# First batch's x in seven pieces, tables and weights held behind it, and other transfer figures in the program that orders the instructions

## The chip, the cores and the metric

The kernel runs on one core of one Trainium2 chip. The core has a matrix engine (TensorE, PE in the profile, with its weight loads as PEld), a vector engine (VectorE, DVE), an activation engine (ScalarE, ACT), a general engine (GpSimd, POOL), and a sequencer (SyncE, SP) that issues every transfer of this kernel; sixteen DMA engines move the data. The metric is the time of one execution on the device in microseconds, as the median of the runs.

## The reference

The first half is a dynamic convolution: every position gets a softmax over 7 taps for each of 8 heads, and adds the 7 last rows of x with these weights. The second half is a Fourier mixing (real part of a two-dimensional transform over positions and channels), a normalization and an MLP of width 768.

```python
batch, seq, d_model = (8, 4224, 192)     # x is (8, 4224, 192), weight_gen (8, 4224, 8, 7)
w = softmax over the 7 taps of weight_gen
out = np.einsum('bshk,bskhg->bshg', w, x_unf)        # x_unf: the 7 rows up to s, 8 heads of 24
X = np.fft.fft(np.fft.fft(x, axis=1), axis=2)        # x is now out
u = x + np.real(X)
un = (u - mean) / np.sqrt(var + 1e-06)               # over the 192 channels
ch = np.maximum(un @ w_ch1, 0.0) @ w_ch2             # 192 -> 768 -> 192
return u + ch
```

## The kernel before, in words

A sequence of 4224 positions is laid out as 128 partitions of 33 rows, so that the transform over positions splits into one of 128 and one of 33 points. The tile x_sb holds 45 such rows of 192 channels for one batch: the 33 and, twice, 6 rows that the taps reach back to. All eight batches use the same x_sb, one after another.

For a batch b the work goes through these steps.

- **conv(b).** Softmax of the tap weights (tile w, maxima and sums in wm), then chunk by chunk: chunk 0 to 7 holds four rows (two from the low half of x_sb and two from the high half), chunk 8 one row. A chunk needs 7 products of x rows with weights wp (tiles pr_b_c_k for chunk c and tap k) and their sum u. Products are made by DVE, some by POOL (POOL_TAPS) and some by ACT (ACT_TAPS). In batch 0 the sums of chunks 0, 1, 3, 5 and 7 are made by PE, which multiplies each product with the identity into a PSUM tile pa; these products share three buffers (tag g2). The other chunks are added by POOL. POOL then folds u into sm, PE multiplies sm with the table f1 (pg), DVE makes gt of it, and gt is written to DRAM (g_d).
- **transform(b)** reads g_d back (g2, printed as g), multiplies it with the tables te and to (pp), and copies the result to pq. **mix(b, g)** multiplies pq with the table cs (eo) and adds it to u.
- **norm(b, g)** normalizes a group g of four rows (un), splits it into two halves of 16 bits (hl), and has it transposed by a DMA (ht<-hl, from group 3 of batch 0 on). From batch 1 on, a second DMA copies 64 partitions of it to the other half of the partitions (hd<-ht, 64 KB).
- **mlp(n)** with n = 9b + g: the first products ph = ht x w1, in 16-bit parts. In the middle of a group come products with only 64 rows of w1l, which use ht and hd side by side. Behind them relu (hh), the second products po = hh x w2, and the addition to u that is written out.

For batch 0, x comes in the pieces of X_PIECES (line 32): a row (a0, a1, b0, b1) stands for two transfers of rows a0 to a1 and b0 to b1, and need_x(c) issues the next rows of the list until chunk c has what it needs. In batch 0 the program asks for x of chunk 8 and 0 first, then for the rest of the weights w, then for chunks 1 and 3, and then load_consts issues the tables f1, te, to, cs and some zeros; load_weights, the MLP's weights, comes behind conv(0).

That order is not what the chip sees. The code records all instructions on a tape, and plan(tape) puts them in an order for each engine: it walks through all of them with a cost for each (cost), a wire that all transfers share, the tiles' buffers, and the places that the program gave them, several times forward and back, and keeps the best walk. In cost, a transfer (lane "sp") has three numbers: the time that SP is busy with it, the time until it is done, and the time that it takes on the wire; the walk adds up the last of them in `wire`. A hold (`held(op)`) tells the planner that what is recorded under it comes behind op on op's engine; it is no wait on the data. emit writes the instructions out in the order found; each engine works through its list in order, and waits where an operand or a buffer isn't ready. All instructions carry the line of emit, 408, so they are told apart by their tiles.

Of the kernel before, what the change touches and what calls it, by code (L numbers as in the profile page):

```python
# [28 lines left out]
NC = 8  # L29
KW = 144  # L30
XR = 45
X_PIECES = [(0, 7, 45, 45), (7, 9, 36, 45), (9, 13, 32, 36), (13, 17, 28, 32), (17, 21, 24, 28), (21, 24, 24, 24)]
TRI = 4
QUICK = 3
PAIRED = 9
# [13 lines left out]
POOL_TAPS = {(0, 0): (5, 6), (0, 1): (5, 6), (0, 3): (6,), (1, 0): range(7), (1, 1): range(7)}  # L49
DVE_ADDS = {(1, c): 1 for c in range(2, NC)}  # L50
HOLD3 = 3
WIRE = 0.7

F32_GROUPS = 7
ACT_ROWS = 4
# [136 lines left out]
def cost(op):  # L192

    lane, reads, writes = op.lane, op.reads, op.writes
    count = lambda ap: int(np.prod([n for _, n in ap.ap[1:]]))
    out = writes[0]
    n = max(map(count, reads + writes))
    if lane == "pe":
        n = count(out)
        t = 2 * max(112 if 64 < n <= DH else 56, 0.855 * n) if reads[0].dtype == F32 else max(55.8, 0.417 * n + 2.4)  # L200
        if op.visit:
            return t / 2, t + 178
        return t, t + 178
    if lane == "sp":
        if op.kw.get("transpose"):
            return 1450, 2000 + 1.2 * n, 1.09 * n
        size, run = BYTES[out.dtype], min(together(ap) for ap in reads + writes)
        return 400, 2000 + WIRE * count(out) * size, out.ap[0][1] * count(out) / run * (0.5 + 0.0023 * run * size)
    if lane == "dve":
        t = 150 + (6.27 if op.call == "reciprocal" else 1.042) * n + (60 if len(reads) == 3 and n < 512 else 0)  # L210
        return t - 83, t
    if lane == "pool":
        t = 183 + (1.92 if out.dtype == F16 else 2.13) * n
        return t - 45, t
    t = 190 + (0.833 if out.ap[-1][0] == 1 else 1.666) * n + 90 * (len(reads) - 1)
    return (t + 100, t + 90) if len(writes) > 1 else (t - 95, t)


def plan(tape):
# [51 lines left out]
    def walk(rank, rows, back=False):  # L271

        to, left = (before, after) if back else (after, before)
        left, ready, span = [len(n) for n in left], [0.0] * len(ops), [None] * len(ops)
        uses = {name: len(set(users[name])) for name in row_of}
        ends, placed, heads = defaultdict(float), {}, {row: 0 for row in rows}
        spare = {row: [(-1e3, i) for i in range(homes[names[0]].bufs)] for row, names in rows.items()}
        free, waiting = {lane: 0.0 for lane in HOP}, {lane: set() for lane in HOP}
        order, table, wire = [], None, 0.0
        half, stays = None, defaultdict(int)  # L280
        taken, wanted = defaultdict(int), {}
        for v in visits:
            stays[v] += 1
        door = set() if back else {span[0] for span in enters.values()}
        for k, n in enumerate(left):
            if n == 0:
                waiting[lanes[k]].add(k)

        def claim(name):

            kind = homes[name].use
            if kind == "fft" and taken["fft"] >= FFT:
                return BANKS
            group = family[name]
            return sum(n for g, n in wanted.items() if g != group)

        def opens(k):

            t = ready[k]
            for name in tiles[k]:  # L300
                if name not in placed:
                    row = row_of[name]
                    if back or row != SHARED:
                        while rows[row][heads[row]] in placed:
                            heads[row] += 1
                        if rows[row][heads[row]] != name:
                            return None
                    if not spare[row] or (row == SHARED and not back and len(spare[row]) <= claim(name)):
                        return None
                    t = max(t, min(spare[row])[0] + HOP[lanes[k]] + (ROOM if row == SHARED else 0))  # L310
            if k in door:
                if len(spare[SHARED]) < 3:
                    return None
                t = max(t, sorted(spare[SHARED])[2][0] + HOP["pe"] + ROOM)
            return t

        for _ in ops:
            at = [(max(free[lane], t), rank[k], k) for lane, ks in waiting.items()
                  for t, k in ((opens(k), k) for k in ks) if t is not None]
            if not at:  # L320
                return None
            if half and stays[half]:
                at = [a for a in at if lanes[a[2]] != "pe" or visits[a[2]] == half] or at
            now = min(at)[0]
            lane = next(lane for lane in HOP if any(t == now and lanes[k] == lane for t, _, k in at))
            k = min((r, k) for t, r, k in at if t == now and lanes[k] == lane)[1]
            if kinds[k] and kinds[k] != table:
                now, table = now + 1283, kinds[k]
            if lane == "pe":
                if visits[k] != half:  # L330
                    now, half = now + VISIT, visits[k]
                stays[half] -= 1
            waiting[lane].remove(k)
            order.append((now, k))
            busy, done, *load = costs[k]
            free[lane], end = now + busy, now + done
            if load and not back:
                wire = max(wire, now + 1000) + load[0]
                end = max(end, wire + 1000)
            span[k] = now, end  # L340
            for name in tiles[k]:
                row = row_of[name]
                if name not in placed:
                    spot = min(spare[row])
                    placed[name] = spot[1]
                    if row == SHARED:
                        taken[homes[name].use] += 1
                        group = family[name]
                        if group in groups:
                            if group not in wanted:  # L350
                                wanted[group] = 6
                            wanted[group] -= 1
                            if not wanted[group]:
                                del wanted[group]
                    spare[row].remove(spot)
                uses[name] -= 1
                ends[name] = max(ends[name], end)
                if not uses[name]:
                    spare[row].append((ends[name], placed[name]))
                    if row == SHARED:  # L360
                        taken[homes[name].use] -= 1
            for j, sync in to[k].items():
                loose = lanes[j] == lane and (lane == "pe" or not sync)
                ready[j] = max(ready[j], now if loose else end + HOP[lane if back else lanes[j]] + (SLACK if lanes[j] != lane else 0))
                left[j] -= 1
                if left[j] == 0:
                    waiting[lanes[j]].add(j)
        return max(end for _, end in span), span, order, placed
# [91 lines left out]
def tile_dynconv_fnet_mlp(  # L460
# [12 lines left out]
    real, nc = tc.nc, Tape()  # L473
# [236 lines left out]
    def conv(b):  # L710
# [13 lines left out]
        def need_x(c):  # L724
            need = {r + k + (0 if r < NT else K - 1) for r in rows_of(c) for k in range(K)}
            while not rows_x.issuperset(need):
                a0, a1, b0, b1 = next(pieces)
                for lo, hi in ((a0, a1), (b0, b1)):
                    if lo < hi:
                        nc.sync.dma_start(x_sb[:, lo:hi, :], x[b, :, lo:hi, :])  # L730
                        rows_x.update(range(lo, hi))

        def need_taps(c):
# [14 lines left out]
        if b == 0:  # L748
            with held(loads[0].ins):
                need_x(NC)  # L750
            with held(tops[0].ins):
                nc.vector.memset(x_sb[:, 7:37:29, 0:1], 0.0)
            first = len(nc.ops)
            need_x(0)
            holds.append((first + 1, 1e9, nc.ops[first]))
            tap_step(0, 4)
            need_x(1)
            need_x(3)
            load_consts()
            if -1 in WARM:  # L760
                keep_warm(pst("fft", [P, P], F32, "warm_x"), WARM[-1])
        groups = [(NC, 0), (1, 2), (3, 4), (5, 6), (7,)] if b == 0 else [(c,) for c in range(NC + 1)]
# [191 lines left out]

    state, us, products = {}, {}, []
    last_tile, last_pg, last_product, last_fold, last_gt, last_g2, last_pp = {}, {}, {}, {}, {}, {}, {}
    last_pq, last_mix, last_up, g2_load = {}, {}, {}, {}
    pending = {}
    total = B * NG

# [234 lines left out]
    last_word, last_split, last_lo, last_bn, last_ph, scales = [], [], {}, {}, {}, []  # L1195
    add(0.0, 1.0, conv(0))
    run(0.5)
    loaded = load_weights()
    run()
    def queue(ins, *calls):  # L1200
        with held(ins):
# [115 lines left out]
```

## Time and profile before

| | us |
|---|---|
| three runs | 1092.83, 1090.03, 1091.94 |
| median | 1091.94 |
| the profiled execution | 1091.01 |
| its span, first to last instruction | 1089.2 |
| VectorE busy | 952.3 (87%) |
| GpSimd busy | 871.4 (80%) |
| ScalarE busy | 789.3 (72%) |

The page also tells that 128.67 MB go through the one DMA queue that SP feeds, and that the DMA engines are busy 44.7% of the span. In the first of 40 slices (27 us) they move 296 GB/s, in the mean 120.

A row of the timeline has a start, a duration, an engine, an operation with its tiles (written<-read, buffer numbers left out), shapes and a count; in brackets stands how long the engine was idle before it and what ended that. Where several alike follow one another they are merged into one row. Spans of one engine can overlap a little, since it begins an instruction before the last one is through. The chain of waits is the path that ended last, followed back from the end; a DMA in it lasts from its issue to its landing. The windows give busy times within a stretch, the clock granted to TensorE (1.00 is full) and what the DMA engines moved.

### The profile page before, as it was taken

How to read it: one execution, taken by the hardware profiler on the slowest of the kernel's cores; microseconds unless marked ns; L12 is line 12 of the kernel's file. 1: busy time of each engine (PE TensorE's matmuls, PEld its weight loads, DVE VectorE, ACT ScalarE, POOL GpSimd, SP SyncE). 2: the span in 40 equal slices, each digit the busy share in tenths (PEclk: the TensorE clock that was granted, in tenths of full speed). 3: DMA queues.
4: the chain of work that ended last, by engine and by line, in shares of the span. 5: the costliest groups of instructions: out<-in, count | busy, mean ns of one | idle time of the engine just before them, and what ended most of it. 6: DMA issues, size and time to landing. Idle time of an engine off the chain costs nothing.

```text
span 1089.2 us, 23832 instructions
## 1 busy us (share of the span) xinstructions
PE 1064.2 (98%) x8596; PEld 807.7 (74%) x8596; DVE 952.3 (87%) x1737; ACT 789.3 (72%) x2385; POOL 871.4 (80%) x759
## 2 busy tenths in 40 slices
PE   7899999999999999999999999999999999999998
PEld 5467788886767867687778777687768877786777
DVE  7999998889999998999999999999999998345443
ACT  4575877568874887678886787778786888589842
POOL 4979899799989999799979999799969999102200
PEclk8999999999999999999999999999999999999999
DMA  8554145615484346714564356614554333612311
GB/s 296 158 147 109 31 110 173 157 40 143 101 210 108 83 118 189 153 57 140 129 183 111 98 115 205 146 58 129 147 142 112 79 68 76 147 51 72 90 54 48
DMA packets 166125, 130.20 MB, mean 120 GB/s; under 512 B 119533, under 2 KB 142710, under 8 KB 166006
## 3 DMA queue, kind: packets, MB, share of 16 engines
q1 hardware_dynamic: 166006, 128.67, 44.7%
q8 instruction: 68, 1.11, 0.4%
q14 instruction: 51, 0.42, 0.1%
HBM read 60.38 MB, written 39.43 MB: 92 GB/s over the span
## 4 chain that ended last, share of the span: by engine, by line
PE 54%; DVE 16%; POOL 15%; issue 7%; ACT 4%; DMA 3%; SPq 0%; DVEq 0%; POOLq 0%; ACTq 0%
PE po L408 22%; PE ph L408 22%; POOL u L408 12%; DVE pr L408 5%; PE eo L408 3%; PE pp L408 3%; DVE u L408 3%; DVE wp L408 2%; PE pg L408 2%; PE pa L408 2%; DVE hh L408 2%; ACT junk L408 1%; POOL hl L408 1%; POOL sm L408 1%; DMA g<-g_d 1%
## 5 line engine op out<-in xcount | busy, mean ns | idle before, releaser
L408 POOL TENSOR_TENSOR u<-u,pr 128x768 f32<-128x768 f32 (+1 forms) x396 | 655.9, 1677 | 18.8 <-DVE pr L408 6.9
L408 PE MATMUL po<-w2h,hh 128*128 128x192 f16 x2832 | 423.1, 247 | 1.8 <-DVE hh L408 1.3
L408 PEld LDWEIGHTS <-hh 128*128 128x128 f16 x4248 | 366.1, 99 | 44.2 <-DVE hh L408 1.9
L408 PE MATMUL ph<-ht,w1h 128*128 128x512 f16 (+1 forms) x1296 | 389.7, 362 | 2.1 <-DMA ht<-hl 1.7
L408 DVE TENSOR_TENSOR pr<-x_sb,wp 128x768 f32<-128x768 f32 (+1 forms) x409 | 349.4, 879 | 21.6 <-POOL u L408 17.0
L408 PE MATMUL po<-w2l,hh 128*128 128x192 f16 x1416 | 347.8, 246 | 0.0
L408 ACT ACTIVATE hh<-ph 128x512 f16<-128x512 f32 (+2 forms) x400 | 220.4, 590 | 113.3 <-PE ph L408 82.1
L408 DVE SCALAR_TENSOR_TENSOR hh<-ph,hh 128x512 f16<-128x512 f32 (+1 forms) x358 | 234.1, 680 | 60.1 <-ACT hh L408 59.9
L408 PE MATMUL ph<-ht,w1l 128*128 128x512 f16 (+2 forms) x696 | 230.2, 358 | 0.0
L408 PEld LDWEIGHTS <-w1h 128*128 128x128 f16 x1296 | 127.4, 99 | 109.7 <-issue 25.9
L408 POOL TENSOR_TENSOR hl<-un,hl 128x512 f16<-128x512 f32 (+1 forms) x138 | 116.9, 860 | 73.6 <-issue 40.7
L408 ACT ACTIVATE un<-u,rs 128x192 f32<-128x192 f32 x264 | 126.6, 538 | 23.5 <-POOL rs L408 16.5
L408 ACT ACTIVATE junk<-u,st 128x192 f16<-128x192 f32 x252 | 114.2, 453 | 4.7
L408 ACT ACTIVATE junk<-u 128x192 f16<-128x192 f32 x252 | 91.1, 362 | 28.4 <-DVE u L408 25.1
L408 PEld LDWEIGHTS <-w1l 128*128 128x128 f16 (+1 forms) x864 | 64.1, 97 | 53.5 <-issue 18.0
L408 DVE SCALAR_TENSOR_TENSOR u<-po,isc,u 128x384 f32<-128x384 f32 (+1 forms) x122 | 73.1, 599 | 22.2 <-PE po L408 22.0
L408 PE MATMUL eo<-cs_sb,pq 97*128 97x97 f32 x544 | 88.2, 273 | 0.3 <-ACT pq L408 0.2
L408 PEld LDWEIGHTS eo<-cs_sb,pq 97*128 97x128 f32 x544 | 79.2, 191 | 8.1 <-DVE hh L408 1.2
L408 POOL TENSOR_TENSOR sm<-u 128x382 f32<-128x382 f32 (+1 forms) x128 | 75.7, 608 | 5.8 <-ACT u L408 5.8
L408 ACT COPY pq<-pp 97x204 f32<-97x204 f32 (+3 forms) x176 | 47.2, 314 | 37.4 <-PE pp L408 33.8
L408 PE MATMUL po<-w2f,hh 128*128 128x192 f32 x336 | 74.3, 327 | 0.0
L408 DVE TENSOR_TENSOR u<-u,eo 128x380 f32<-128x380 f32 (+3 forms) x160 | 71.5, 491 | 0.6
(92 smaller groups left out, 1168.8 us busy)
## 6 DMA issues: line engine op xcount, KB each, us to landing
out_dram<-u SPq DMA_DIRECT2D x64, 384.0 KB
x_sb<-in_x_dram SPq DMA_DIRECT2D x48, 384.0 KB
x_sb<-in_x_dram SPq DMA_DIRECT2D x8, 864.0 KB
g<-g_d SPq DMA_DIRECT2D x40, 162.0 KB
g_d<-gt SPq DMA_DIRECT2D x32, 195.0 KB
g_d<-gt SPq DMA_DIRECT2D x32, 189.0 KB
g<-g_d SPq DMA_DIRECT2D x40, 144.0 KB
w<-in_weight_gen_dram SPq DMA_DIRECT2D x6, 924.0 KB
```

The source lines that it names most:

```text
L408: ins = getattr(getattr(nc, op.engine), op.call)(*map(found, op.args), **{n: found(a) for n, a in op.kw.items()}).ins
```

## The change

```diff
-X_PIECES = [(0, 7, 45, 45), (7, 9, 36, 45), (9, 13, 32, 36), (13, 17, 28, 32), (17, 21, 24, 28), (21, 24, 24, 24)]
+X_PIECES = [(0, 7, 45, 45), (7, 9, 36, 40), (9, 9, 40, 45), (9, 13, 32, 36), (13, 17, 28, 32), (17, 21, 24, 28), (21, 24, 24, 24)]
...
-WIRE = 0.7
+WIRE = 0.5
...
         if op.kw.get("transpose"):
-            return 1450, 2000 + 1.2 * n, 1.09 * n
+            return 1450, 2000 + 1.2 * n, 1.15 * n
         size, run = BYTES[out.dtype], min(together(ap) for ap in reads + writes)
-        return 400, 2000 + WIRE * count(out) * size, out.ap[0][1] * count(out) / run * (0.5 + 0.0023 * run * size)
+        return 400, 1750 + WIRE * count(out) * size, out.ap[0][1] * count(out) / run * (1.35 + 0.0035 * run * size)
...
-                wire = max(wire, now + 1000) + load[0]
-                end = max(end, wire + 1000)
+                wire = max(wire, now + 440) + load[0]
+                end = max(end, wire + 1200)
...
-                        nc.sync.dma_start(x_sb[:, lo:hi, :], x[b, :, lo:hi, :])
+                        last_x[b] = nc.sync.dma_start(x_sb[:, lo:hi, :], x[b, :, lo:hi, :])
...
-            need_x(1)
-            need_x(3)
-            load_consts()
+            need_x(NC - 1)
+            with held(last_x[0].ins):
+                load_consts()
...
-    loaded = load_weights()
+    with held(last_x[0].ins):
+        loaded = load_weights()
```

There are three parts. The nine rows 36 to 44 come as four and five. In batch 0 all pieces of x are recorded ahead of the tables, and tables and weights are held behind the last piece recorded, rows 21 to 23. And the planner has other costs for transfers, by which it orders every instruction of the kernel anew; the work itself is the same. The list of pieces holds for all eight batches.

What the instructions' order makes of it is shown at three places. The first is the start of SP's list; a transfer 128x1728 is nine rows of x (864 KB), 128x960 five, 128x768 four (384 KB), 128x576 three, 128x1344 seven; f is the table f1, w the tap weights. Before:

```order
L408 DMA w_22_67<-in_weight_gen_dram 128x2x280
L408 DMA x_sb_71<-in_x_dram 128x1344
L408 DMA x_sb_71<-in_x_dram 128x384
L408 DMA x_sb_71<-in_x_dram 128x1728
L408 DMA w_22_67<-in_weight_gen_dram 128x1288
L408 DMA x_sb_71<-in_x_dram 128x768 x2
L408 DMA f_sb_105<-in_f_dram 128x128
L408 DMA f_sb_105<-in_f_dram 128x512
L408 DMA x_sb_71<-in_x_dram 128x768 x2
L408 DMA f_sb_105<-in_f_dram 128x768
L408 DMA x_sb_71<-in_x_dram 128x768 x2
L408 DMA x_sb_71<-in_x_dram 128x576
```

The same place of SP's list in the change:

```order
L408 DMA w_22_67<-in_weight_gen_dram 128x2x280
L408 DMA x_sb_71<-in_x_dram 128x1344
L408 DMA x_sb_71<-in_x_dram 128x384
L408 DMA x_sb_71<-in_x_dram 128x768
L408 DMA w_22_67<-in_weight_gen_dram 128x1288
L408 DMA x_sb_71<-in_x_dram 128x960
L408 DMA x_sb_71<-in_x_dram 128x768 x2
L408 DMA x_sb_71<-in_x_dram 128x576
L408 DMA f_sb_108<-in_f_dram 128x128
L408 DMA x_sb_71<-in_x_dram 128x768 x2
L408 DMA f_sb_108<-in_f_dram 128x512
L408 DMA f_sb_108<-in_f_dram 128x768
```

Four of the nine rows go ahead of the larger part of w, five behind it; rows 21 to 23 went from the end of x to the middle. The first pair of 128x768 was rows 32 to 35 and then 9 to 12, and is now rows 9 to 12 and then 32 to 35.

The second place is DVE's list from the first product of batch 0 on. pr_0_0 is chunk 0's product of tap 0, pr_8_1 chunk 8's of tap 1, and so on; the reductions and the product of w with itself belong to the softmax of the larger part of w. Before:

```order
L408 TENSOR_TENSOR pr_0_0_32_152<-x_sb_71,wp_8_26_116 128x768
L408 TENSOR_TENSOR pr_8_1_33_165<-x_sb_71,wp_8_26_116 128x192
L408 TENSOR_TENSOR pr_8_2_35_172<-x_sb_71,wp_8_26_116 128x192
L408 TENSOR_TENSOR pr_0_1_36_176<-x_sb_71,wp_8_26_116 128x768
L408 TENSOR_REDUCE wm_24_188<-w_22_67 128x184
L408 TENSOR_TENSOR pr_8_3_37_205<-x_sb_71,wp_8_26_116 128x192
L408 TENSOR_TENSOR w_22_67<-w_22_67,wm_24_188 128x1288
L408 TENSOR_TENSOR pr_0_2_38_218<-x_sb_71,wp_8_26_116 128x768
L408 TENSOR_TENSOR pr_8_4_39_227<-x_sb_71,wp_8_26_116 128x192
L408 TENSOR_TENSOR pr_8_5_41_231<-x_sb_71,wp_8_26_116 128x192
L408 TENSOR_TENSOR pr_0_3_42_236<-x_sb_71,wp_8_26_116 128x768
L408 TENSOR_REDUCE wm_24_188<-w_22_67 128x184
```

DVE's list from the same product on, in the change:

```order
L408 TENSOR_TENSOR pr_0_0_32_133<-x_sb_71,wp_8_26_116 128x768
L408 TENSOR_TENSOR pr_8_1_33_143<-x_sb_71,wp_8_26_116 128x192
L408 TENSOR_TENSOR pr_8_2_35_149<-x_sb_71,wp_8_26_116 128x192
L408 TENSOR_REDUCE wm_24_154<-w_22_67 128x184
L408 TENSOR_TENSOR w_22_67<-w_22_67,wm_24_154 128x1288
L408 TENSOR_TENSOR pr_0_1_36_191<-x_sb_71,wp_8_26_116 128x768
L408 TENSOR_TENSOR pr_8_3_37_196<-x_sb_71,wp_8_26_116 128x192
L408 TENSOR_TENSOR pr_0_2_38_199<-x_sb_71,wp_8_26_116 128x768
L408 TENSOR_TENSOR pr_8_4_39_208<-x_sb_71,wp_8_26_116 128x192
L408 TENSOR_TENSOR pr_8_5_41_212<-x_sb_71,wp_8_26_116 128x192
L408 TENSOR_REDUCE wm_24_154<-w_22_67 128x184
L408 TENSOR_TENSOR pr_0_3_42_234<-x_sb_71,wp_8_26_116 128x768
```

Both reductions and the subtraction (w<-w,wm) moved ahead of a product of chunk 0. On POOL, chunk 0's product of tap 5 went behind two additions to u of chunk 8, and chunk 3's product of tap 6 went ahead of the last two additions to u of chunk 2. On PE, one pair of transform products (pg of chunk 4) went from the end of chunk 5 into the run of chunk 7.

The third place is SP's list in batch 2, from the transpose of group 1 to the copy hd of that group. Before:

```order
L408 DMA_TRANSPOSE ht_2_1_854_4578<-hl_2_1_853_4523 128x12x128
L408 DMA out_0_dram<-u_1_8_442_1905 128x192
L408 DMA x_sb_0_71<-in_x_dram 128x1728
L408 DMA x_sb_0_71<-in_x_dram 128x768
L408 DMA hd_2_1_855_4636<-ht_2_1_854_4578 64x4x128
```

SP's list in the change, from two transfers ahead of the same transpose:

```order
L408 DMA x_sb_0_71<-in_x_dram 128x768
L408 DMA out_0_dram<-u_1_8_442_1933 128x192
L408 DMA_TRANSPOSE ht_2_1_854_4609<-hl_2_1_853_4546 128x12x128
L408 DMA x_sb_0_71<-in_x_dram 128x768
L408 DMA hd_2_1_855_4661<-ht_2_1_854_4609 64x4x128
```

Between transpose and copy there were 96 KB of output and 1248 KB of x, and there are now 384 KB of x. The five rows of the split piece (128x960) went further up, with 7 to 8, ahead of the transpose of group 0. On PE, 13 products of the MLP stand between the first use of ht and the first use of hd in that group; now 13 narrow ones of the second products (128x192) stand there as well. For group 4 of the same batch the queue between transpose and copy grew from 1152 KB to 1980 KB (two pieces of 384, one of 288 and the weights w of batch 5, 924 KB), and on PE from 13 wide products and 2 of pg to 13 wide and 32 narrow ones.

More of the change, by code (lines that the diff above doesn't have):

```diff
@@ L956, in tile_dynconv_fnet_mlp @@
     last_tile, last_pg, last_product, last_fold, last_gt, last_g2, last_pp = {}, {}, {}, {}, {}, {}, {}
-    last_pq, last_mix, last_up, g2_load = {}, {}, {}, {}
+    last_pq, last_mix, last_up, g2_load, last_x = {}, {}, {}, {}, {}
     pending = {}
```

## The prediction

> **What bounds the kernel now.** I read the busy times of the page first, then the windows that cut the span at 104 us (the first product of the MLP starts at 104.0), then TensorE's waits behind that cut. Columns of a window row: stretch, its length, busy time of PE, PEld, DVE, ACT, POOL with instruction counts, granted TensorE clock, DMA share, GB/s. A row of waits has the total, the number of times and the longest.
>
> ```profile
> PE 1064.2 (98%) x8596; PEld 807.7 (74%) x8596; DVE 952.3 (87%) x1737; ACT 789.3 (72%) x2385; POOL 871.4 (80%) x759
> 0.00:104.00 104.00, 90.45 (x444) 63.45 (x445) 95.43 (x202) 57.02 (x227) 81.57 (x71) 0.97 0.60 186
> 104.00:1089.20 985.20, 973.71 (x8152) 744.24 (x8151) 856.85 (x1536) 732.32 (x2159) 789.88 (x689) 1.00 0.44 113
> PE ph L408 <- DMA hd<-ht: 2.7, 1, 2.7
> PE ph L408 <- DMA ht<-hl: 1.7, 2, 0.9
> PE po L408 <- DVE hh L408: 1.3, 1, 1.3
> PE pp L408 <- DMA g<-g_d: 0.7, 1, 0.7
> ```
>
> Two stages with two limits. Behind 104 us PE is busy 973.71 of 985.20 us, and the change adds or removes no product, so there only the gaps can move: four groups of waits, 6.4 us, of which one single wait for a DMA is 2.7. Ahead of 104 us VectorE (DVE) is the fullest engine (95.43 of 104), so whatever DVE waits for early postpones the first product, and with it all 985 us behind it. The prediction therefore has two terms: DVE's waits in the first stage, and PE's DMA waits in the second.
>
> **First stage, before.** The rows below are the chain's DMA piece, two window rows of 1 us, then the timelines of DVE, ACT, POOL and PE (start, length, instruction, count, in brackets the idle time before it and what ended it), and last the one wait of DVE between 60 and 104 us.
>
> ```profile
> 4.80 5.24 DMA x_sb<-in_x_dram
> 8.00:9.00 1.00, 0.00 (x0) 0.00 (x0) 0.70 (x2) 1.00 (x5) 0.51 (x2) 1.00 0.94 361
> 9.00:10.00 1.00, 0.00 (x0) 0.00 (x0) 0.00 (x0) 1.00 (x6) 0.00 (x0) 0.95 1.02 421
> 8.38 0.35 DVE L408 TENSOR_TENSOR u<-x_sb,wp 128x192 f32<-128x192 f32 x1
> 10.07 2.35 DVE L408 TENSOR_TENSOR pr<-x_sb,wp 128x768 f32<-128x768 f32 x4 [1.34 <-DMA x_sb<-in_x_dram]
> 12.34 1.50 DVE L408 TENSOR_REDUCE wm<-w 128x184 f32<-128x1288 f32 x1
> 14.00 1.49 DVE L408 TENSOR_TENSOR w<-w,wm 128x1288 f32<-128x1288 f32 x1
> 15.40 1.48 DVE L408 TENSOR_TENSOR pr<-x_sb,wp 128x768 f32<-128x768 f32 x3
> 18.04 0.95 DVE L408 TENSOR_TENSOR pr<-x_sb,wp 128x768 f32<-128x768 f32 x1 [1.16 <-PE pa L408]
> 18.91 1.50 DVE L408 TENSOR_REDUCE wm<-w 128x184 f32<-128x1288 f32 x1
> 21.70 1.31 DVE L408 RECIPROCAL wm<-wm 128x184 f32<-128x184 f32 x1
> 43.16 4.41 DVE L408 TENSOR_TENSOR pr<-x_sb,wp 128x768 f32<-128x768 f32 x5 [0.71 <-PE pa L408]
> 65.56 0.95 DVE L408 TENSOR_TENSOR pr<-x_sb,wp 128x768 f32<-128x768 f32 x1 [0.77 <-PE pa L408]
> 12.63 3.19 ACT L408 ACTIVATE pr<-x_sb,wa 128x24 f32<-128x24 f32 x15 [1.08 <-DMA x_sb<-in_x_dram]
> 15.73 1.26 ACT L408 ACTIVATE w<-w 128x1288 f32<-128x1288 f32 x1
> 10.21 1.50 POOL L408 TENSOR_TENSOR pr<-x_sb,wq 128x768 f32<-128x768 f32 x1 [1.70 <-DMA x_sb<-in_x_dram]
> 26.62 9.38 POOL L408 TENSOR_TENSOR u<-u,pr 128x768 f32<-128x768 f32 x5
> 39.96 1.48 POOL L408 TENSOR_TENSOR pr<-x_sb,wq 128x768 f32<-128x768 f32 x1
> 41.49 9.61 PE L408 MATMUL pa<-pr,ident 128*128 128x384 f32 x28 [0.53 <-POOL pr L408]
> DVE pr L408 <- PE pa L408: 0.8, 1, 0.8
> ```
>
> **Term 1, the split piece of the first batch.** The nine-row piece (864 KB) lands at 4.80 + 5.24 = 10.04, and DVE, done with u at 8.73, stands until 10.07. The four-row piece brings what the first product needs; the 480 KB behind it (0.49 MB) take 1.2 to 1.4 us at the 361 to 421 GB/s of the window rows, so it lands near 8.7 and the wait shrinks from 1.34 to about 0. The rest is a walk down DVE's new order. The remaining weights, now queued ahead of the last five rows, land 0.49 MB earlier, near 10.4; DVE has by then made one 768-wide product (0.87 apart, from 4.41 for five) and two narrow ones, and starts the reduction at 10.45 instead of 12.34, the subtraction at 11.85 instead of 14.00. Two things eat into this. The five rows still land near 11.6, so POOL's product of tap 5 starts at 11.75, not 10.21, ends at 13.25, and PE, which takes the taps in order, has a hole there. And the rows that ACT's second group of 16 needs (32 to 36) are now the second of two 384 KB pieces, so 1.0 us later (13.6); eight of them (3.19/15 = 0.21 each) and the exponential (1.26) end at 16.5, and DVE's second reduction starts at 16.6 instead of 18.91. Then PE's buffers hold the fourth tap until about 18.0, as they hold it until 18.04 now, behind the reduction instead of ahead of it; reduction and product have changed places, and the reciprocal starts near 20.3 instead of 21.70: **-1.4 us**.
>
> Two later waits of DVE change too. At 43.16 it waits 0.71 for PE, and the PE row shows for what: POOL's product of chunk 3, made at 39.96 behind the additions to u of chunk 2 (9.38 for five, 1.88 each). In the new order POOL makes it two additions sooner, so this wait goes: -0.7. At 65.56 it waits 0.77 for PE in chunk 7, where the new PE order has one more pair of transform products (about 0.65) ahead of the buffer that DVE needs: +0.4, since not all of it need show. Behind 65.56 DVE has no other wait up to 104 (the last row), its work there is the same, so the shift reaches the first product. Term 1: -1.4 - 0.7 + 0.4 = **-1.7 us**. From both sides: all four waits of the rows gone and nothing in their place gives -1.34 - 1.16 - 0.71 - 0.77 = -4.0; if the hole on PE takes everything back and the third wait grows, +0.4.
>
> The Trainium skill, "DMA: Bandwidth & Descriptors", section "Bandwidth", speaks against such a split: it wants 1 MiB per transfer and measures 138 GB/s at 64 KB against 341 at 1 MB. The window rows disagree where several pieces are queued behind one another (361 and 421 GB/s). By the page the four rows (0.39 MB) alone would cost 1.2 to 2.8 us, term 1 would lie between -1.7 and about -0.3, and the sum at most 1.4 later.
>
> **Holding tables and weights behind x.** The hold names the piece that stands last in the program (rows 21 to 23), and the ordering program issues that one fifth from the end of x, so three of the four transfers of the first table still go ahead of the last two pieces of x. PE's timeline has the first use of that table:
>
> ```profile
> 23.23 0.49 PE L408 MATMUL pg<-u,f_sb 128*128 128x192 f32 x2
> ```
>
> I price the hold at 0: the queue moved 361 to 421 GB/s throughout, so a table that changes places with 768 KB of x comes about 2 us later, well before 23 us. The ends are the 1.34 us that a DMA wait cost here, either way.
>
> **Term 2, the same split in the later batches.** X_PIECES serves all eight. The rows: SP's issues (x_sb's two are 864 and 384 KB), the chain's piece, windows, and PE around the wait.
>
> ```profile
> 380.61 1.16 SPq L408 DMA_DIRECT2D x_sb<-in_x_dram  x2
> 381.87 0.62 SPq L408 DMA_DIRECT2D hd<-ht  x1
> 381.87 6.16 DMA hd<-ht
> 384.00:385.00 1.00, 1.00 (x6) 0.32 (x4) 1.00 (x4) 1.00 (x4) 1.00 (x3) 1.00 0.93 372
> 386.00:387.00 1.00, 0.00 (x0) 0.00 (x0) 1.00 (x3) 0.48 (x3) 1.00 (x2) 1.00 0.06 9
> 388.80:392.20 3.40, 3.40 (x18) 2.44 (x18) 3.36 (x7) 1.61 (x6) 3.40 (x5) 0.50 0.29 57
> 383.59 0.81 PE L408 MATMUL ph<-ht,w1h 128*128 128x512 f16 x3
> 384.24 0.38 PE L408 MATMUL ph<-ht,w1l 128*128 128x512 f16 x1
> 384.98 0.39 PE L408 MATMUL ph<-ht,w1l 64*128 64x512 f16 x1
> 388.07 0.39 PE L408 MATMUL ph<-hd,w1l 64*128 64x512 f16 x1 [2.70 <-DMA hd<-ht]
> 392.51 0.33 PE L408 MATMUL po<-w2h,hh 128*128 128x192 f16 x2
> 392.68 0.25 PE L408 MATMUL po<-w2l,hh 128*128 128x192 f16 x1
> ```
>
> hd is a copy of 64 KB, yet it lands 6.16 us after its issue. The windows say why: x moves at 372 GB/s until 386, then almost nothing moves for 2 us and hd lands at 388.02. So 4.1 us are the queue ahead and 2.0 its own. PE stands 2.70 us for it, and afterwards its clock is granted at 0.50 for 3.4 us: another 1.7. In the new order one piece of 384 KB stands between transpose and copy instead of 1248 KB of x: 0.39 MB at 372 GB/s is 1.1, plus 2.0, so hd would land 3.1 us behind its issue, at 385.0, where PE wants it at 385.4; and PE has 13 more products of 128x192 to do first (0.085 apart, 1.1 us). The wait goes, and the slow clock with it: **-2.7 - 1.7 = -4.4 us**. From both sides: -4.4, and 0 if the new order lays another wait in the same place.
>
> The Trainium skill, "TensorE: Matmul & The Clock Gate", section "What's actually happening", lets the clock fall only behind an idle window of about 3.4 us. Here 2.70 us were enough, so the row decides; by the page term 2 would be -2.7 and the sum 1.7 later.
>
> **Term 3, the new figures for transfers** rewrite the order of everything behind. The other waits of the second stage (6.4 - 2.7 = 3.7) are dealt anew; I carry them at the same size. One place is worse to see: between transpose and copy of batch 2's group 4 the queue now holds 1980 KB (1152 before). 2.03 MB at 372 GB/s is 5.4, plus 2.0; PE has 13 wide products (0.216 apart) and 32 narrow ones, 5.5 us, to fill it. The wait is at most 1.9 us if nothing of the queue has moved by the issue; I take half, **+0.9**. Ends of the term: -3.7 (all waits gone), and +5 (this wait in full with its 1.7 of slow clock, and one more like the 1.3).
>
> **Sum.** The profiled execution took 1091.01 us (span 1089.2 and 1.8 around it): 1091.01 - 1.7 - 4.4 + 0.9 = 1085.8. The median of the three runs is 0.93 above that execution, so on its scale **1086.7 us**.
>
> **Rivals.**
> - The first stage gives nothing: POOL's late tap 5 and ACT's late rows take the whole start back. For it: the buffers that hold DVE at 18.04 are freed by PE, and PE waits for POOL there. Against: DVE's reductions move up by 1.9 and 2.3 us whatever PE does. 1086.7 + 1.7 = 1088.4.
> - hd waits elsewhere: the queue of 1980 KB gives back 1.9 + 1.7 instead of 0.9. For it: its bytes; against: twice the products to cover it. It decides when PE reaches hd under 7.4 us behind the issue. 1086.7 + 2.7 = 1089.4.
> - Slower: SP issues in order, and x pieces now stand ahead of the transpose of each batch's first group (rows 40 to 44 and 7 to 8 of batch b+1 ahead of ht of group 0). If such a piece must wait for its last reader, the transpose behind it waits too and PE starves; the ht waits of the waits' row (0.9 the longest) are of that kind. It decides when SP stands over 2 us there. Six batches at 0.9 and 1.7 of slow clock each are 15.6: 1086.7 + 15.6 = 1102. Against: rows 40 to 44 are read by chunks 0 to 2 alone, so they come free before rows 7 and 8, which stand at the same place already.
>
> **How the numbers follow.** The forecast has 0.50, the first rival 0.22, the second 0.18, the third 0.10. A measurement of this kernel tells about 0.3% (3.3 us) from no change, so faster means under 1088.7. The forecast is nearly all there (0.47), the first rival just over half (0.12), the second a quarter (0.04): faster 0.63. The rest of the first three, 0.27, is no change, the third 0.10 slower. The low end is the forecast with term 1 at -3.2 and term 3 at -2.5, so 1086.7 - 1.5 - 3.4 = 1082; the upper end leaves the third rival out and takes term 3 at +5 with the first rival: 1086.7 + 1.7 + 4.1 = 1092.5, and one more microsecond for the spread of the runs shown (2.8): 1093.5.
>
> **What would show it.** DVE's first wide product near 8.75 with no DMA wait ahead, its second reduction near 16.6, the reciprocal near 20.3, the first product of the MLP near 102.3 instead of 104.0. PE's waits behind that: no 2.7 for hd in batch 2, no stretch at half clock behind 300 us, and at most 1.9 at group 4 of batch 2. If the first product starts at 104 again, term 1 is wrong; if the waits for hd, ht and g sum to more than the 5.1 of now, term 2 went into term 3.

## The result, and the profile after

| | before, us | the change, us |
|---|---|---|
| median (lowest to highest) of five runs each | 1091.94 (1090.03 to 1092.83) | 1102.46 (1099.15 to 1105.41) |
| profiled execution | 1091.01 | 1099.67 |
| its span | 1089.2 | 1097.8 |

The change is slower: ratio 1.0096, 95% interval 1.0068 to 1.0124. All five of its runs lie above the range that was predicted (1082.0 to 1093.5).

The page's busy times, the two windows that meet at 104 us, and TensorE's waits behind 104 us (total, number, longest), in the profile of the change:

```profile
PE 1065.3 (97%) x8596; PEld 808.5 (74%) x8596; DVE 961.5 (88%) x1737; ACT 786.1 (72%) x2385; POOL 871.5 (79%) x759
0.00:104.00 104.00, 91.20 (x451) 64.09 (x451) 96.59 (x209) 59.60 (x232) 86.17 (x74) 0.95 0.59 186
104.00:1097.80 993.80, 974.06 (x8147) 744.40 (x8146) 864.87 (x1529) 726.48 (x2155) 785.34 (x686) 0.99 0.43 112
PE mr_w L408 <- DVE mx_w L408: 7.4, 1, 7.4
PE po L408 <- DVE hh L408: 4.4, 7, 1.8
PE pp L408 <- DMA g<-g_d: 2.5, 3, 1.4
PE pp L408 <- DVE hh L408: 1.2, 2, 0.8
PE po L408 <- ACT junk L408: 0.4, 1, 0.4
PE ph L408 <- DMA ht<-hl: 0.3, 1, 0.3
PE ph L408 <- DVE hh L408: 0.2, 1, 0.2
```

Behind 104 us PE was idle for 993.80 - 974.06 = 19.74 us, before for 985.20 - 973.71 = 11.49. The 8.25 between them are nearly all of the 8.6 by which the span grew. The wait for hd is gone; a single new wait, of mr_w for mx_w, is longer than the four groups of waits that the prediction counted in before (6.4 together). It is no wait for a DMA: the two tiles belong to the scale of the MLP's second weights (w2). DVE reduces each third of w2 to a maximum per partition (three columns of mx_w), cuts these 128x3 numbers to their exponents with a bit mask, and takes the largest; one product on PE (mr_w) carries that to all partitions. Here are DVE, POOL and PE around it, and then windows of 2 us:

```profile
178.70 0.55 DVE L408 TENSOR_REDUCE mx_w<-w2f 128x1 f32<-128x384 f32 x1
179.09 8.85 POOL L408 TENSOR_TENSOR u<-u,pr 128x768 f32<-128x768 f32 x5
179.16 0.94 DVE L408 TENSOR_TENSOR pr<-x_sb,wp 128x768 f32<-128x768 f32 x1
180.02 8.90 DVE L408 TENSOR_SCALAR mx_w<-mx_w 128x3 int32<-128x3 int32 x1
187.89 1.00 POOL L408 TENSOR_TENSOR sm<-u 128x382 f32<-128x382 f32 x1
188.95 0.16 DVE L408 TENSOR_REDUCE mx_w<-mx_w 128x1 f32<-128x3 int32 x1
189.16 0.80 PE L408 MATMUL mr_w<-ident,mx_w 128*128 128x128 f32 x2 [7.43 <-DVE mx_w L408]
184.00:186.00 2.00, 0.00 (x0) 0.00 (x0) 2.00 (x1) 0.00 (x0) 2.00 (x2) 1.00 0.00 0
186.00:188.00 2.00, 0.00 (x0) 0.00 (x0) 2.00 (x1) 0.00 (x0) 2.00 (x3) 0.70 0.00 0
190.00:192.00 2.00, 2.00 (x7) 1.30 (x7) 2.00 (x10) 0.07 (x1) 1.30 (x1) 0.50 0.74 147
```

The mask works on three numbers per partition and takes 8.90 us. It shows as busy time of DVE, not as a wait, which is why DVE's share rose while its work is the same. Six instructions of POOL stand beside it without a gap, five additions to u and a fold, and the mask ends at 188.92, 0.03 behind the last of them. From 182 us until then PE and ACT do nothing, and TensorE's clock falls to 0.50. Before, the same mask stood right behind its reduction:

```profile
169.28 0.31 DVE L408 TENSOR_SCALAR mx_w<-mx_w 128x3 int32<-128x3 int32 x1
```

The first stage, by contrast, looked as forecast, on DVE and on PE:

```profile
8.62 1.48 DVE L408 TENSOR_TENSOR pr<-x_sb,wp 128x768 f32<-128x768 f32 x3
10.02 1.50 DVE L408 TENSOR_REDUCE wm<-w 128x184 f32<-128x1288 f32 x1
15.48 1.50 DVE L408 TENSOR_REDUCE wm<-w 128x184 f32<-128x1288 f32 x1
19.13 1.31 DVE L408 RECIPROCAL wm<-wm 128x184 f32<-128x184 f32 x1
96.97 4.64 PE L408 MATMUL tr<-ident,un 128*128 128x128 f32 x16 [2.14 <-ACT un L408]
101.67 0.59 PE L408 MATMUL ph<-ht,w1h 128*128 128x512 f16 x1
```

The wait for x is gone and, in this execution, the first product of the MLP starts 2.3 us earlier. But PE's first transposes (tr) run at half clock: 4.70 us from tr to that product, where before it took 3.50.

### The profile page after: what moved, and what is told of

It reads as the page before. It is cut to its first block, busy times and chain, and to the rows that moved or that the text cites. A ratio compares the mean times of both kernels' runs of the same rounds, so it can differ in the third digit from the quotient of the medians.

```text
span 1097.8 us, 23882 instructions
## 1 busy us (share of the span) xinstructions
PE 1065.3 (97%) x8596; PEld 808.5 (74%) x8596; DVE 961.5 (88%) x1737; ACT 786.1 (72%) x2385; POOL 871.5 (79%) x759
## 4 chain that ended last, share of the span: by engine, by line
PE 57%; DVE 21%; POOL 10%; issue 5%; DMA 5%; SPq 1%; ACT 1%; DVEq 0%; POOLq 0%
PE po L408 24%; PE ph L408 24%; DVE pr L408 8%; POOL u L408 8%; PE eo L408 3%; DVE u L408 3%; DVE hh L408 3%; PE pp L408 3%; PE pg L408 2%; DVE wp L408 2%; DMA g<-g_d 1%; POOL hl L408 1%; DVE mx_w L408 1%; DMA ht<-hl 1%; PE tr L408 1%
## 5 line engine op out<-in xcount | busy, mean ns | idle before, releaser
L408 PE MATMUL po<-w2h,hh 128*128 128x192 f16 x2832 | 417.4, 246 | 4.7 <-DVE hh L408 4.4
```

The lines of the kernel that those rows point to most:

```text
L408: ins = getattr(getattr(nc, op.engine), op.call)(*map(found, op.args), **{n: found(a) for n, a in op.kw.items()}).ins
```

## The experiments

**One part alone.** What of the change makes the mask late?

```diff
# e1_pieces: before, with
+X_PIECES = [(0, 7, 45, 45), (7, 9, 36, 40), (9, 9, 40, 45), (9, 13, 32, 36), (13, 17, 28, 32), (17, 21, 24, 28), (21, 24, 24, 24)]
# e2_figures: before, with the change's figures
+WIRE = 0.5
+            return 1450, 2000 + 1.2 * n, 1.15 * n
+        return 400, 1750 + WIRE * count(out) * size, out.ap[0][1] * count(out) / run * (1.35 + 0.0035 * run * size)
+                wire = max(wire, now + 440) + load[0]
+                end = max(end, wire + 1200)
# e3_pieces_hold: the change, with before's lines in these five places
```

> The kernel before with the seven pieces of x alone; order of loads, holds and planner figures as before. Theory 1 (the loss of the change is one stall: DVE's exponent mask of w2, 128x3, held 8.9 us beside an unbroken row of GpSimd additions, 7.4 us of it and 3.4 us of half clock on PE; the new figures put the mask there): no such stall, since the old figures leave the mask right behind its reductions; the first stage gains 2 to 3.5 us, about 1089. Theory 2 (the pieces themselves cost, in the transfers of the later batches): 1095 or more. Theory 3 (any new order of this planner costs some us, whatever the edit): 1095 to 1105 with waits in many places.

> The kernel before with the new figures for transfers alone. Theory 1: the mask of w2 stands late again, 18 instructions behind its first reductions, and is held if GpSimd is in a row of additions there: 1100 to 1103 with an 8 to 9 us mask, and 1092 without. Theory 2 (pieces): as before, 1092. Theory 3: 1095 to 1105 with no single wait over 3 us.

> The change with the old figures put back, so pieces, order of loads and holds without the figures. Theory 1: no long mask, about 1088 to 1090, as e1_pieces within 2 us. Theory 2: 1095 or more. Theory 3: 1095 to 1105.

Ratios to before on the same chip (before 1090.87 us): e1 1.0017 (1.0000 to 1.0035), e2 1.0057 (1.0041 to 1.0073), e3 1.0017 (0.9997 to 1.0037). The mask in e2, with the product behind it, and in e3:

```profile
179.10 8.89 DVE L408 TENSOR_SCALAR mx_w<-mx_w 128x3 int32<-128x3 int32 x1
188.24 0.80 PE L408 MATMUL mr_w<-ident,mx_w 128*128 128x128 f32 x2 [7.46 <-DVE mx_w L408]
```

```profile
169.30 0.33 DVE L408 TENSOR_SCALAR mx_w<-mx_w 128x3 int32<-128x3 int32 x1
18.00 0.95 DVE L408 TENSOR_TENSOR pr<-x_sb,wp 128x768 f32<-128x768 f32 x1 [2.58 <-PE pa L408]
```

The new figures alone put the mask beside POOL's row and bring over half of the loss. With the old figures it stays at 0.33. The second row of e3 is the wait that the prediction's first rival names: DVE's wait for PE's buffers grew from 1.16 to 2.58, since POOL's product of tap 5 waited for its later rows (it starts at 12.13 us, at 10.21 before). So split and holds, under the old figures, give nothing that can be told from no change; the 2 to 3.5 us that e1 was expected to gain, and e3's 1088 to 1090, did not come.

**The change with the mask in another form.** The order of every engine stays, because the edit is made in emit, behind the planner: only the instruction is written differently.

```diff
# e4_mask3, in emit: the change, with the mask of w2 as three instructions
+    if op.call == "tensor_scalar" and op.writes[0].tensor.name.startswith("mx_w2") and op.writes[0].ap[-1][1] == 3:
+        return [dict(args, out=args["out"][:, j:j + 1], in0=args["in0"][:, j:j + 1]) for j in range(3)]
# e5_again: the change itself
# e6_mask3_isc, in emit: e4, with the 128x1 product of the two scales on ScalarE
+    if op.call == "tensor_tensor" and name.startswith("isc"):
+        return [("scalar", "mul", [kw["out"], kw["in0"], kw["in1"]], {})]
```

> The change, every engine's order kept, but the exponent mask of w2 issued as three instructions of 128x1 instead of one of 128x3 (the same values). The rows show that one-column instructions of this kind (191.53 and 191.76 us) take 0.14 us beside GpSimd's additions. Theory 1 with the shape as the trigger: the three take under 0.5 us together, PE's wait of 7.4 us and the half clock behind it go, 1102.5 - 10.8 = 1091.7. If integer masks are held whatever their width: three times 1.8 us or the same 8.9, 1099 or more. Theory 3: the waiting moves to later places, 1098 to 1102.

> The change itself once more, beside the kernel before and the two runs after it on the same chip. If the stall of DVE's mask belongs to the order and not to one execution, the mask takes 8.9 us again at about 180 to 184 us. If the first stage depends on how late the last DMA engine delivers (in the run e4_mask3, with the same order there, the larger part of w was complete at 11.93 us and the first transpose by PE began at 99.83, in the profile of the change at 9.92 and 96.97), this run falls between or beside the two: first transpose 97 to 100. Time 1100 to 1103.

> As e4_mask3, and the product of the two scales (isc, 128x1, two SBUF operands), which there was held 6.3 us beside GpSimd's row, made by ScalarE; all else in the order of the change. Theory 1 (both instructions share something with GpSimd that the others, with an operand in PSUM, don't need): PE's wait of 3.25 us at 195.81 and its half clock go too; 1097.5 - 3.25 - 1.7 = 1092.5, within 1.5 us. Rival (DVE is simply behind there and PE waits for it whatever these two do): 1096 to 1098, with a wait of 2 us or more between 185 and 215.

e4 came out at 1.0056 (1.0038 to 1.0075). The mask is cured and something else is late; these are e4's DVE and PE:

```profile
184.29 0.27 DVE L417 TENSOR_SCALAR mx_w<-mx_w 128x1 int32<-128x1 int32 x3
188.73 6.30 DVE L417 TENSOR_TENSOR isc<-sc_w,sc_w 128x1 f32<-128x1 f32 x1
195.81 0.58 PE L417 MATMUL ph<-ht,w1h 128*128 128x512 f16 x1 [3.25 <-DVE w2l L417]
```

As 128x1 the mask passes, three times in 0.27 us. But the next product of the same helper, isc, one number per partition, stands 6.30 us (0.33 before, 1.80 in the change) and ends 0.02 behind an addition of POOL. It is held in the same way, and PE waits 3.25 for what DVE makes behind it, and runs at half clock for 3.41 from 195.26. So e4 showed a second victim instead of the full gain.

On another chip (before 1090.92) the change itself gave 1103.74, again 1.0096 (1.0066 to 1.0126), with the mask at 8.93 us and the wait at 7.49. e6, with both out of the way, gave 1094.46, 1.0025 (1.0011 to 1.0040): 9.3 us less, and half a microsecond above the range expected. In e6's trace PE has no wait over 1 us between its first transposes and 274 us. What e6 still has is the slow clock at the first transposes, 6.83 us long (two stretches of 3.41 us follow much later, from 333.5 and 586.1):

```profile
97.48 5.12 PE L420 MATMUL tr<-ident,un 128*128 128x128 f32 x16 [2.14 <-ACT un L420]
96.00:104.00 8.00, 6.46 (x20) 3.55 (x21) 6.39 (x32) 3.94 (x9) 8.00 (x6) 0.62 0.00 0
```

**The gap ahead of the first transposes.** The program has 16 products that nobody needs (warm_eo, two instructions each) in PE's list to bridge that gap. In the change the gap is 2.14 instead of 1.29. The figures alone don't do that: in e2 it is 1.42, and the transposes run at full speed, which fits its smaller loss. In e1 and e3 it is 1.28. Here is e2's row:

```profile
98.73 3.19 PE L408 MATMUL tr<-ident,un 128*128 128x128 f32 x16 [1.42 <-DVE rs L408]
```

Eight more of these products fill the gap:

```diff
# in emit; e7_warm: on e6; e9_warm_only: on the change
+        if name.startswith("warm_eo"):
+            tape.warm = getattr(tape, "warm", 0) + 1
+            return [(op.engine, op.call, args, kw)] * (9 if tape.warm == sum(WARM_EO) else 1)
```

> As e6_mask3_isc, with eight more dummy products of 128x128 on PE (1.8 us) ahead of the first transpose by PE, where PE sat idle 2.1 us and then ran 6.8 to 10.2 us at half clock. If the gap starts the half clock: no stretch at 0.5 between 95 and 115, 3.4 to 5.1 us less than e6_mask3_isc, about 1088. If PE is throttled there for another reason, or waits for what stands behind: the same as e6_mask3_isc, and if the dummies come in the way up to 2 us more.

> The change with the eight dummy products ahead of the first transpose by PE alone; mask and scale product as in the change. If the half clock behind that gap is a loss of its own: no stretch at 0.5 between 95 and 115, 3.4 to 5.1 us below the change, so 1098 to 1100, about where e2_figures stood, with the 8.9 us mask still there. If it only comes together with the stall (what it gives is lost again at 190): 1102 or more.

e7: 1089.97 us, 0.9988 (0.9971 to 1.0005), 4.5 less than e6 on the same chip. e9: 1.0073 (1.0048 to 1.0098). e7's PE and the windows of the same stretch:

```profile
95.21 3.76 PE L423 MATMUL warm_eo<-ident 128*128 128x128 f32 x32
99.34 3.19 PE L423 MATMUL tr<-ident,un 128*128 128x128 f32 x16 [0.36 <-ACT un L423]
96.00:104.00 8.00, 7.33 (x49) 5.49 (x48) 7.97 (x42) 4.14 (x10) 8.00 (x6) 1.00 0.01 3
```

With the gap at 0.36 the clock is full. Half of 6.83 us is 3.4 of the 4.5; whether e6's two later slow stretches, which e7's trace doesn't have, went by the same repair isn't shown. e9 has the full clock at the transposes too and keeps the mask at 8.94 us; it came out 0.0023 below the change, but the two intervals overlap, so what the gap costs rests on e6 and e7. The two repairs together take the change from 1.0096 to 0.9988, so within these intervals holds and gap make up the whole loss.

**Does before gain from the same repairs?** If so, e7's time is no merit of the change.

```diff
# e11_before_repaired: before, with the edits of e4, e6 and
+            return [(op.engine, op.call, args, kw)] * (6 if tape.warm == sum(WARM_EO) else 1)
```

> The kernel before, its order kept, with the three repairs of e7_warm: mask in three columns, scale product on ScalarE, five dummy products ahead of the first transpose by PE (gap there 1.3 us). Its mask lost 0.16 us and its scale product 0.18, and its profiles show no half clock there: 1090 to 1091.5, the same as the kernel before; 1088 or less if the gap of 1.3 us starts the half clock in other executions of it.

1089.01 us, 0.9981 (0.9964 to 0.9998), the fastest version of all, though by less than 0.3%, and a little below the 1090 to 1091.5 expected. Its trace has only 0.5 us of waiting for hd and no half clock near 388; whether that comes from the repairs or from the one execution isn't shown. Repaired alike, the two orders can't be told apart (0.9988 and 0.9981, the intervals overlap): but for these two accidents the change shows neither gain nor loss.

**What holds an instruction of DVE beside POOL.** The next three append a probe to before, behind its last work, so their times are longer by the probe and tell nothing. POOL makes a row of 128x768 additions; DVE makes reductions of the same size to time itself, and then issues the probe.

```diff
# e12_probe3, at the end of emit: rows of 12 additions over 2 or 6 tiles, probe behind 3 to 8 reductions
+        for j in range(12):
+            own = spare[j % tiles]
+            add("pool", nc.gpsimd.tensor_tensor(out=own, in0=own, in1=b, op=ALU.add))
+        for j in range(wait):
+            add("dve", top(16 + j))
+        add("dve", run())
# e10_probe2: rows of 6 over 1, 2 or 6 tiles, probe behind one reduction
# e8_probe: the same, all sums from one tile, written to it or to several
```

> The kernel before, with eight probes behind its end: GpSimd makes six additions 128x768 in a row (1.8 us each), and 1 us into the row DVE issues one instruction. Theory 1: held to the row's end (8 us or more) are the mask 128x3 and the product 128x1 of two SBUF operands, also 128x768 and the mask 128x4; not held (0.15 and 0.9 us) are the mask 128x1 and the reduction. If only narrow instructions are held, the product 128x768 takes 0.95 us. If the hold lasts for one GpSimd instruction only, 1 to 1.8 us instead of 8; additions that don't depend on one another (probes 2 and 5) tell whether the row's chain matters. The time of the whole is 90 to 100 us above the kernel before.

> The kernel before with eight other probes behind its end: six GpSimd additions over two tiles in turn, over one, or over six, and 1 to 2 us into the row one DVE instruction. In e8_probe every addition waited for the one ahead (0.08 us between them) and the mask was let in behind the first. If it is the gap that lets DVE in: over two or six tiles the additions overlap and the mask 128x3 and the product 128x1 are held to the row's end, 7 to 10 us; over one tile 1 to 1.8 us. If DVE is let in behind any GpSimd instruction: 2 us at most in all eight, and the 8.9 us of the kernel have another reason. The mask 128x1 takes 0.15 in any case.

> The kernel before with probes behind its end once more: rows of twelve GpSimd additions (1.76 us apart, 21 us) over two tiles in turn or over six, and DVE's mask 128x3 or product 128x1 issued 2.6 to 7 us into the row. In e8_probe and e10_probe2 every probe came in the first addition of a row, and the addition behind it waited for DVE or for the one before it. If an addition that waits for GpSimd's own work of two steps earlier, as in the kernel, doesn't let DVE in, the probes in rows over two tiles are held to the row's end, 14 to 18 us. If DVE is let in behind any addition here too, each takes 0.3 to 2 us, and why the kernel's mask was passed over five times stays open.

e8's probes on DVE, by form:

```profile
1087.47 1.14 DVE L427 TENSOR_SCALAR x_sb<-x_sb 128x3 int32<-128x3 int32 x1
1109.80 0.14 DVE L427 TENSOR_SCALAR x_sb<-x_sb 128x1 int32<-128x1 int32 x1
1121.21 1.12 DVE L428 TENSOR_TENSOR x_sb<-x_sb 128x1 f32<-128x1 f32 x1
1143.65 1.80 DVE L428 TENSOR_TENSOR x_sb<-x_sb 128x768 f32<-128x768 f32 x1
1155.54 0.94 DVE L429 TENSOR_REDUCE x_sb<-x_sb 128x1 f32<-128x768 f32 x1
1166.94 1.13 DVE L427 TENSOR_SCALAR x_sb<-x_sb 128x4 int32<-128x4 int32 x1
```

Masks of 128x3 and 128x4 and products with both operands in SBUF, however small, wait for the end of the addition that is under way (1.1 us here). The mask of 128x1 and the reduction run beside it at their usual 0.14 and 0.94. The Trainium skill, "SBUF — State Buffer", section "Who interferes with whom", has this rule: VectorE and GpSimd share a pair of ports; a tensor_tensor from two SBUF inputs and a tensor_scalar in its two-port mode contend for it with GpSimd, the later of the two waits, and reductions don't contend. For the two-port mode the Trainium skill, "Advanced Engine Details and Errata", section "2x-2p Requirements", wants an even or an equal odd size above 1, so 128x1 is out. All forms here agree. It fits the kernel as well: most of DVE's work in that stretch has an operand in PSUM, and these two instructions have none; the product of x_sb and wp at 179.16, with wp in PSUM, took its 0.94 us beside POOL.

But in e8 the probe is let in behind one addition, and the kernel's mask was passed over five times, up to the end of the row. e10 tried whether additions that overlap, having separate tiles, close the door: they don't, seven probes again got in behind the first (0.83 to 1.55 us), and the 128x1 mask took its 0.14. That theory fell. e12 moved the moment of the issue:

```profile
1092.05 1.18 DVE L427 TENSOR_SCALAR x_sb<-x_sb 128x3 int32<-128x3 int32 x1
1114.27 17.64 DVE L427 TENSOR_SCALAR x_sb<-x_sb 128x3 int32<-128x3 int32 x1
1158.37 15.94 DVE L427 TENSOR_SCALAR x_sb<-x_sb 128x3 int32<-128x3 int32 x1
1177.81 0.20 DVE L427 TENSOR_SCALAR x_sb<-x_sb 128x3 int32<-128x3 int32 x1
1244.92 14.18 DVE L428 TENSOR_TENSOR x_sb<-x_sb 128x1 f32<-128x1 f32 x1
```

So it happens by itself, away from this kernel: four of the eight probes got in within 1.2 us, four were passed over until the row was at its end, 14.2 to 17.6 us later. The four that were passed over had been issued at most 0.13 us ahead of an addition's end, the others at least 0.17 ahead. That doesn't settle it: the kernel's mask was issued about 0.9 ahead of one, and was passed over in each of the four executions that have it in this place. What decides who is let in stays open.

## Why the prediction was wrong, point by point

**Term 3 is the step that failed.** "The other waits of the second stage (6.4 - 2.7 = 3.7) are dealt anew; I carry them at the same size." No row stood behind "the same size", and the one place that was worked out was a wait for a DMA, where transfers changed; but an order that is new for all engines also brings instructions of DVE beside other instructions of POOL. The mask went from behind its reduction to beside POOL's row: 7.4 us of wait, and 6.83 us of half clock from 186.79, of which 2.4 lie inside the wait, so the remaining 4.5 cost some 2.2. With 9.6 us together, this one place is more than the +5 at which the range ended the term. The change from DMA waits to DVE's shows in the rest too: hh took 1.3 before and 4.4 now. The longest of its seven waits, 1.76, shows why, on DVE and PE of the change:

```profile
337.42 3.54 DVE L408 TENSOR_TENSOR pr<-x_sb,wp 128x768 f32<-128x768 f32 x4
340.87 1.28 DVE L408 SCALAR_TENSOR_TENSOR hh<-ph,hh 128x512 f16<-128x512 f32 x2
341.62 0.34 PE L408 MATMUL po<-w2h,hh 128*128 128x192 f16 x2 [1.76 <-DVE hh L408]
```

Four products of the convolution stand ahead of an hh that PE needs at once; the clock falls for 3.41 us behind it, at 343.81. These waits came with every new order that was run: 4.0 to 4.4 in nine profiles (e1, e2, e3 and the six of the change's order), 1.3 in all five of before's order. The one place that I did work out, group 4 of batch 2 at +0.9, has no wait at all.

**Term 2 was right.** The 2.70 for hd and the half clock at 388 are gone, and the DMA waits that were put down as its test are g 2.5 and ht 0.3, in all 2.8, below the 5.1 of the test. Other executions agree: these three waits sum to 2.5 to 4.3 in six profiles of the change's order and to 5.1 to 8.7 in five of before's, 4.2 less in the mean. The gain was real, and smaller than the new waits on DVE: those for hh alone take 2.9 of it back.

**Term 1 looked right in one execution and isn't a gain.** Forecast 8.75, 16.6, 20.3 and 102.3, measured 8.62, 15.48, 19.13 and 101.67. But other executions of the same first stage differ, as e5's DVE and PE show:

```profile
12.28 1.50 DVE L408 TENSOR_REDUCE wm<-w 128x184 f32<-128x1288 f32 x1 [2.12 <-DMA w<-in_weight_gen_dram]
101.73 4.40 PE L408 MATMUL tr<-ident,un 128*128 128x128 f32 x16 [2.15 <-ACT un L408]
```

The larger part of w, complete at 9.92 in the first profile, was complete here at 12.26, and the transposes started 4.8 us later, at 101.73, outside the 97 to 100 expected. In six profiles of the change's order (the change, e4, e5, e6, e7, e9) the transposes start at 96.97, 99.83, 101.73, 97.48, 99.34 and 100.24, mean 99.3; in five of before's (before, e8, e10, e11, e12) at 100.51, 99.07, 98.85, 98.62 and 99.86, mean 99.4, so no gain shows. In the records of the single DMA engines, the first of the sixteen has its share of w through at 9.3 to 9.6 in all six, the last at 9.92 to 12.26, and the order of the six is the order in which their transposes start (9.92, 10.48, 11.12, 11.93, 12.06 and 12.26 against 96.97, 97.48, 99.34, 99.83, 100.24 and 101.73). I read a time of arrival off the queue's mean rate; the slowest engine sets it. The first rival (the first stage gives nothing) is what holds, but not by its own way alone: w is late first, and DVE waits for it (2.12 in e5); the rows behind it are late with it, so tap 5, the rival's cause, starts at 13.60 in e5 against 11.45 in the first profile.

The gap ahead of the transposes was in no step. It came with the change's order too: 2.14 instead of 1.29 us without work on PE, and half clock at the transposes in all four profiles with such a gap (the change, e4, e5, e6: 6.83 to 10.24 us long).

**The third rival** had the measured time, 1102, and not the mechanism: it had PE starve for late transposes, and PE's waits for ht are 0.3 us in all. Its number agreed by chance.

The span's +8.6 is thus +8.25 of PE's idle time behind 104 us and +0.35 of busy time: there the products that had begun 2.3 us earlier are set against some 2.7 us more of slow clock (half of 0.88, 4.5 and 3.41 us behind 104, against half of 3.41 before).

## What to carry to other kernels

A change of a planner's figures is a change of every engine's order: look for what newly stands beside what, above all for short VectorE instructions with all operands in SBUF next to long rows of GpSimd, when PE waits for their result. Such an instruction shows as a long busy row with tiny operands; single columns for the mask and ScalarE for the product took the hold away here. And one execution of a stage that depends on when a DMA's slowest engine is done says little: compare its start over several profiles before counting a gain.

## What the runs showed of the hardware that was not expected

- One VectorE instruction of 128x3 numbers stood for 8.90, 8.89, 8.93 and 8.94 us (the change, e2, e5, e9) behind a whole row of GpSimd instructions, and for up to 17.64 in e12, though the same mask of the first weights took 0.15 with GpSimd idle (the change, at 66.35). That an instruction waits for the one under way could be expected; that the next one is let in ahead of it, five to ten times over, could not.
- TensorE's clock came back only after 3.41, 6.83 or 10.24 us, one, two or three times the same stretch. Gaps of 2.13 to 2.15 us ahead of the transposes brought it in four of four profiles, gaps of 1.28 to 1.42 in one of seven (e1, 10.24 us), and gaps of 0.36 or less in none of three (e7, e9, e11). The Trainium skill, "TensorE: Matmul & The Clock Gate", section "What's actually happening", gives a free-running window of about 3.4 us, which agrees with these lengths, and wants a whole window idle ahead of a fall, which doesn't: here less than two thirds of it were enough four times.
- A transfer of 644 KB, behind pieces of x and in the same place of the queue, was complete at 9.92 us in one execution and at 12.26 in another, with its first DMA engine done at 9.3 to 9.6 in both.
